# Local heads in 96-query blocks, strided heads by residue, and X in token order for an attention + MLP kernel

## The chip, the cores and the metric

The kernel runs on one core of a Trainium2 chip. The metric is the time of one execution on the device in microseconds (us). Every time below is a median of several executions, with the lowest and highest beside it. The engines are named as the profile names them: PE is TensorE (matmuls), PEld its loads of the stationary operand, DVE is VectorE, ACT is ScalarE, POOL is GpSimd, and SP is SyncE, which only issues DMAs here.

Executions of the kernel before differ by up to about 3% on one chip. Each execution has a state: it is called slow when it is over 1.5% above the fastest one of the same kernel.

## The reference

Eight batches of 8 heads, 576 positions, head width 64. Heads 0 to 3 see a local window of 32 positions, heads 4 to 7 see every 32nd position. The result, 4608 tokens of 512 features, goes through an MLP (512 to 2048 to 512) with a rational activation. It is condensed here to its core, not quoted:

```python
mask_local   = (rel >= 0) & (rel < 32)                      # heads 0..3
mask_strided = (rel >= 0) & (pos_k % 32 == pos_q % 32)      # heads 4..7
attn = softmax(where(mask, q @ k.T / 8, -1e9)) @ v
x = attn.transpose(0, 2, 1, 3).reshape(4608, 512)
h = x @ w_in                                                # 512 -> 2048
P = a0 + a1*h + a2*h*h + a3*h*h*h
Q = 1 + |b0|*|h| + |b1|*h*h
out = (P / (Q + 1e-6)) @ w_out                              # 2048 -> 512
```

## The kernel before

The program records its operations and puts them into a fixed order for each engine. For each batch there are score rounds (`scores`), five attention tiles (`attend`), and then one MLP chunk of 512 tokens (`dense1`, activation, `dense2`, `store`). The last 64 tokens of all eight batches form a ninth chunk.

Attention produces X with tokens on partitions (`XR`). The MLP needs it transposed, with features on partitions and tokens along the free dimension. A transposing DMA does this, tile by tile, into `XT`:

```python
# attend(b), tile T of five
ev = add("SP", (lambda e, dst=dst, x=x: e.dma_start_transpose(dst, x[:, :])),   # dst = XT[b % 2][:, :, 128*T : 128*T+128]
         [o3, wait], 1.25, key - 60, gx, 0.6)
```

The first dense layer then runs four matmuls for each block of 128 hidden features, one for each 128 input features. `r` is the moving operand (512 columns, one a token), and all of them are read in the order in which they lie:

```python
# dense1(c)
for kk in range(NK1):                                    # NK1 = 4
    if c < 8:
        r = XT[c % NXT][:, kk, :]
    else:
        r = XT8[:, kk, :].rearrange("x (n c) -> x n c", c=32)[:, :, 0:16]
    makers.append(mm(psH[hi], Win[:, kk, 128 * f:128 * f + 128], r, kk == 0, kk == NK1 - 1))
```

To get this the kernel keeps the queries of each 128-token tile in the order (residue mod 4, position). The copy of the transposed queries out of PSUM puts them in that order, and `store` undoes it with four DMAs for each tile. The copy of the transposed keys writes `kL` in token order, in steps of 4 elements:

```python
# scores(b), turn_l: queries, then keys
e = [(eng, qL[:, a, 0:512].rearrange("x (t g p) -> x g t p", t=4, g=4),
      lambda ps, a=a: ps[:, a, :].rearrange("x (g t p) -> x g t p", g=4, t=4), 512) for a in range(2)]
e = [(eng, kL[:, :, 0:512].rearrange("x a (p g) -> x a g p", g=4),
      lambda ps: ps.rearrange("x a (g p) -> x a g p", g=4), 1024)]
# ... (cut)
# store(c, m): rows in steps of 4
dst = out[576 * c + 128 * m:576 * c + 128 * m + 128, :].rearrange("(p g) o -> g p o", g=4)
for g in range(4):
    add("SP", (lambda e, dst=dst, osl=osl, g=g: e.dma_start(
        dst[g], OS[osl][32 * g:32 * g + 32, :])), [ev], 0.75, key - 60, go, 0.2)
```

The softmax here doesn't subtract the row's maximum and nothing guards it: scores larger than these inputs give would overflow.

## Time and profile before

| | before |
|---|---|
| median (lowest to highest), 3 runs | 435.72 us (430.99 to 436.88) |
| profiled span, mean granted clock of TensorE | 435.9 us, 0.930 |
| first matmul of the first dense layer | 45.4 us |
| steady stage | 180 to 340 us, about 40 us a chunk (39.7 to 41.9 from start to start between 178 and 300 us) |
| issue of the last 32 stores | 14.9 us |

These are lines of the profile page before. The first gives for each engine its busy time, its share of the span and its instructions. In the others, each digit is the busy share of one fortieth of the span in tenths; PEclk is the granted clock of TensorE in tenths, and DMA is the mean busy share of the 16 DMA engines.

```profile
PE 367.6 (84%) x3417; PEld 175.6 (40%) x3417; DVE 329.0 (75%) x309; ACT 305.4 (70%) x338; POOL 107.4 (25%) x144
...
PE   6751877679996999799989999999999997998760
...
DVE  3421197960599589689996989796989999999920
ACT  2320398926794899789978897879897798849510
...
PEclk9875698969999999999999999999999999899895
DMA  9999998029929923952594265221123101012012
```

The start is thin on PE, DVE and ACT while the DMA engines are nearly full for the first seven slices (76 us); the middle is full on PE, DVE and ACT together, and the end is thin again. So three engines share the steady stage, and the start and the tail are waits.

Two groups of instructions on the page before. The columns are line, engine, operation, written and read tiles, shape and count, then busy us and mean ns of one, then the idle time of the engine before them and what ended it.

```profile
L518 PE MATMUL psH<-XT,Win 128*128 128x512 bf16 x576 | 147.5, 393 | 18.9 <-DMA XT<-XR 16.8
...
L813 ACT ACTIVATE HB<-psH 128x512 bf16<-128x512 f32 x144 | 84.3, 600 | 58.8 <-PE psH L518 57.7
```

The mean of a matmul (393 ns) contains a modelled end and overlaps its neighbours. What it costs in a full stream is read from starts. The PE timeline before, with start, duration, and runs of equal instructions folded:

```profile
305.15 1.03 PE L518 MATMUL psH<-XT,Win 128*128 128x512 bf16 x4
306.02 1.03 PE L518 MATMUL psO<-Wout,T 128*128 128x512 bf16 x4
306.88 1.03 PE L518 MATMUL psH<-XT,Win 128*128 128x512 bf16 x4
```

Four matmuls take 306.02 - 305.15 = 0.87 us, so one takes about 216 ns. The next view is the table of windows. Its columns are the window, its length, the busy us and count of PE, PEld, DVE, ACT and POOL, the granted clock, the DMA share and GB/s.

```profile
180.00:220.00 40.00, 37.25 (x401) 18.66 (x400) 34.74 (x32) 36.40 (x39) 13.23 (x17) 1.00 0.57 78
...
300.00:340.00 40.00, 39.84 (x326) 18.84 (x325) 38.59 (x32) 32.96 (x39) 0.00 (x0) 1.00 0.21 50
```

PE has no slack, and DVE and ACT have little slack. The start is in the chain of waits (start us, us, what), and PE's list of waits (total us, times, longest) gives the sum:

```profile
27.13 8.14 DMA XT<-XR
36.09 9.20 DMA XT<-XR
45.38 6.34 PE psH L518 x16
```

```profile
PE psH L518 <- DMA XT<-XR: 16.8, 4, 7.9
```

Two transposing DMAs in a row hold up the first dense matmul. The median one of the run lands 2.4 us after its issue, and these two take 8.1 and 9.2 us at a time when the DMA engines are nearly full; that the loads delay them is likely, but was not tested. The tail is on SP's timeline:

```profile
419.18 14.93 SPq L874 DMA_DIRECT2D out_dram<-OS  x32
```

Last, the groups of ACT's copies out of PSUM, with shapes kept apart:

```profile
L529 ACT ACTIVATE kL<-psS 128x1024 bf16<-128x1024 f32 x6 | 14.8, 2464 | 1.8 <-PE psS L518 1.8
...
L529 ACT ACTIVATE sT<-psS 128x1024 bf16<-128x1024 f32 x6 | 6.1, 1020 | 0.0
```

Both copies move 1024 elements per partition. The one that writes SBUF in 8-byte steps (`kL`) takes 2.4 times as long as the one that writes in order (`sT`).

### The profile page before, as it was taken

What the parts mean: (1) busy time and instruction counts of PE and PEld (TensorE: products, weight loads), DVE (VectorE), ACT (ScalarE), POOL (GpSimd) and SP (SyncE); (2) the same over time, 40 slices, a digit from 0 to 9 for tenths busy, and PEclk for the clock granted to TensorE, in tenths of its full rate; (3) what the DMA queues carried; (4) which work ended last, traced back from release to release, by engine and by line L of the source; (5) the groups of instructions that cost most, each with busy time, mean ns of one, the idle gap of its engine ahead of it and who ended that gap; (6) DMA issues with size and microseconds to landing.
All of it is one profiled execution on the core that took longest, in us unless ns stands there. A gap on an engine that the chain in (4) does not pass through costs nothing.

```text
span 435.9 us, 7966 instructions
## 1 busy us (share of the span) xinstructions
PE 367.6 (84%) x3417; PEld 175.6 (40%) x3417; DVE 329.0 (75%) x309; ACT 305.4 (70%) x338; POOL 107.4 (25%) x144
## 2 busy tenths in 40 slices
PE   6751877679996999799989999999999997998760
PEld 2330332334552454355435444553454442343320
DVE  3421197960599589689996989796989999999920
ACT  2320398926794899789978897879897798849510
POOL 9985211008208402900580064000000000000000
PEclk9875698969999999999999999999999999899895
DMA  9999998029929923952594265221123101012012
GB/s 130 182 192 166 199 110 108 15 29 96 115 54 127 94 49 47 147 81 50 67 149 74 48 85 69 61 50 26 26 48 85 28 23 48 25 44 54 24 35 64
DMA packets 92260, 34.05 MB, mean 78 GB/s; under 512 B 66112, under 2 KB 87104, under 8 KB 92224
## 3 DMA queue, kind: packets, MB, share of 16 engines
q0 software_dynamic: 62144, 18.37, 42.0%
q1 hardware_dynamic: 30080, 15.16, 16.2%
q8 instruction: 27, 0.44, 0.5%
q14 instruction: 9, 0.07, 0.1%
HBM read 37.17 MB, written 9.44 MB: 107 GB/s over the span
## 4 chain that ended last, share of the span: by engine, by line
PE 49%; DVE 25%; DMA 11%; ACT 9%; issue 3%; SPq 1%; DVEq 0%
PE psH L518 20%; PE psO L518 14%; PE psS L518 10%; DMA XT<-XR 9%; PE psA L518 6%; DVE UU L827 4%; DVE T L852 3%; DVE T L843 3%; DVE T L847 3%; ACT kL L529 2%; DVE XR L749 2%; ACT UU L833 2%; DVE T L845 2%; DVE UU L824 2%; ACT UU L836 2%
## 5 line engine op out<-in xcount | busy, mean ns | idle before, releaser
L518 PE MATMUL psH<-XT,Win 128*128 128x512 bf16 x576 | 147.5, 393 | 18.9 <-DMA XT<-XR 16.8
L518 PE MATMUL psO<-Wout,T 128*128 128x512 bf16 x528 | 133.9, 384 | 8.7 <-ACT OS L917 4.9
L813 ACT ACTIVATE HB<-psH 128x512 bf16<-128x512 f32 x144 | 84.3, 600 | 58.8 <-PE psH L518 57.7
L518 PEld LDWEIGHTS psH<-XT,Win 128*128 128x128 bf16 x576 | 55.0, 100 | 87.0 <-issue 16.3
L833 ACT ACTIVATE UU<-UU,cst 128x2048 bf16<-128x2048 bf16 x36 | 71.5, 1998 | 7.1 <-DVE UU L827 7.0
L518 PEld LDWEIGHTS psO<-Wout,T 128*128 128x128 bf16 x528 | 47.1, 98 | 65.6 <-ACT OS L917 9.1
L836 ACT ACTIVATE UU<-UU 128x2048 bf16<-128x2048 bf16 x36 | 68.5, 1912 | 0.1
L821 DVE TENSOR_SCALAR T<-HB 128x4096 uint16<-128x4096 uint16 (+1 forms) x20 | 22.4, 1121 | 38.6 <-ACT HB L813 38.6
L852 DVE TENSOR_TENSOR T<-T,UU 128x4096 bf16<-128x4096 bf16 (+1 forms) x20 | 41.3, 2063 | 4.0 <-ACT UU L836 4.0
L485 POOL DMA_DIRECT2D vs<-in_v_dram x32 | 27.4, 861 | 63.9 <-PE psA L518 63.5
L847 DVE TENSOR_TENSOR T<-T,HB 128x4096 bf16<-128x4096 bf16 (+1 forms) x20 | 41.4, 2069 | 0.3
L827 DVE TENSOR_TENSOR UU<-UU,T 128x4096 bf16<-128x4096 bf16 (+1 forms) x20 | 41.4, 2069 | 0.3
L843 DVE TENSOR_TENSOR T<-T,HB 128x4096 bf16<-128x4096 bf16 (+1 forms) x20 | 41.3, 2067 | 0.2
L457 POOL DMA_DIRECT2D qn<-in_q_dram x9 | 8.7, 965 | 89.7 <-PE psS L518 88.9
L749 DVE TENSOR_TENSOR XR<-psA,RC 128x512 bf16<-128x512 f32 x40 | 27.4, 686 | 3.2 <-DMA XT<-XR 3.0
L917 ACT ACTIVATE OS<-psO 128x512 f32<-128x512 f32 x33 | 20.0, 606 | 12.7 <-PE psO L518 12.2
L495 POOL DMA_DIRECT2D vt<-in_v_dram x32 | 26.1, 847 | 0.0
L575 ACT ACTIVATE ES<-psS 128x864 bf16<-128x864 f32 (+1 forms) x20 | 17.0, 852 | 12.5 <-PE psS L518 11.0
L840 DVE TENSOR_SCALAR T<-HB,coef 128x4096 bf16<-128x4096 bf16 (+1 forms) x20 | 24.8, 1238 | 0.3
L824 DVE TENSOR_SCALAR UU<-T,coef 128x4096 bf16<-128x4096 bf16 (+1 forms) x20 | 24.6, 1230 | 0.3
L845 DVE TENSOR_SCALAR T<-T,coef 128x4096 bf16<-128x4096 bf16 (+1 forms) x20 | 23.6, 1182 | 0.3
L747 DVE RECIPROCAL RC<-psA 128x8 f32<-128x8 f32 x40 | 8.1, 203 | 20.8 <-PE psA L518 20.7
(111 smaller groups left out, 391.7 us busy)
## 6 DMA issues: line engine op xcount, KB each, us to landing
out_dram<-OS SPq DMA_DIRECT2D x128, 64.0 KB, 1.7
qn<-in_q_dram POOLq DMA_DIRECT2D x7, 512.0 KB, 6.8
kn<-in_k_dram POOLq DMA_DIRECT2D x7, 512.0 KB, 5.8
vs<-in_v_dram POOLq DMA_DIRECT2D x32, 64.0 KB, 6.3
vt<-in_v_dram POOLq DMA_DIRECT2D x32, 64.0 KB, 3.5
Win<-in_moe_w_in_dram POOLq DMA_DIRECT2D x1, 2048.0 KB, 13.4
Wout<-in_moe_w_out_dram POOLq DMA_DIRECT2D x1, 2048.0 KB, 26.2
out_dram<-OS SPq DMA_DIRECT2D x32, 32.0 KB, 1.7
```

Source lines behind the costliest of these rows:

```text
L485: add("POOL", (lambda e, b=b, i=i, h=h: e.dma_start(vs[i][:, h, :, 0:64], v[b, 4 + h, 0:512, :].rearrange("(p g) d -> p g d", g=4))), base ...
L518: return lambda e: e.matmul(out_ap, l, r, start=start, stop=stop, skip_group_check=True)
L749: o3 = add("DVE", (lambda d, rc=rc, x=x: d.tensor_tensor(x.rearrange("x (h d) -> x h d", h=8), psA[:, :, 0:64], rc[:, :, :].to_broadcast([ ...
L813: o2 = add("ACT", (lambda a, hb=hb, hi=hi, fi=fi: a.activation(hb[:, fi, :], psH[hi], AF.Copy)), [o1, hb_free[ig % NHB]], 0.6, key - HOFF)
L824: d2 = add("DVE", (lambda d, gn=gn, u=u, t3=t3: d.tensor_scalar(u[:, 0:gn, :], t3[:, 0:gn, :], b1_ap, b0_ap, op0=Alu.mult, op1=Alu.add)), ...
L827: d3 = add("DVE", (lambda d, gn=gn, u=u, t3=t3: d.tensor_tensor(u[:, 0:gn, :], u[:, 0:gn, :], t3[:, 0:gn, :], op=Alu.mult)), [d2], ctt, ke ...
L833: ln = add("ACT", (lambda a, u=u, sl=sl: a.activation(u[:, sl, :], u[:, sl, :], AF.Ln, bias=cst[:, 0:1], scale=1.0)), [d3, cons], 0.28 + H ...
L836: ex = add("ACT", (lambda a, u=u, sl=sl: a.activation(u[:, sl, :], u[:, sl, :], AF.Exp, scale=-1.0)), [ln], 0.28 + HG * CH * 0.000833, key ...
L843: d5 = add("DVE", (lambda d, gn=gn, hb=hb, t3=t3: d.tensor_tensor(t3[:, 0:gn, :], t3[:, 0:gn, :], hb[:, 0:gn, :], op=Alu.mult)), [d4], ctt ...
L845: d6 = add("DVE", (lambda d, gn=gn, t3=t3: d.tensor_scalar(t3[:, 0:gn, :], t3[:, 0:gn, :], a_ap[1], None, op0=Alu.add)), [d5], cts, key + ...
L847: d7 = add("DVE", (lambda d, gn=gn, hb=hb, t3=t3: d.tensor_tensor(t3[:, 0:gn, :], t3[:, 0:gn, :], hb[:, 0:gn, :], op=Alu.mult)), [d6], ctt ...
L852: d9 = add("DVE", (lambda d, gn=gn, t3=t3, u=u: d.tensor_tensor(t3[:, 0:gn, :], t3[:, 0:gn, :], u[:, 0:gn, :], op=Alu.mult)), [d8, lns], c ...
```

## The change

The intent was to shorten the start, to lighten PE a little in the steady stage, and to store each tile with one DMA. Its parts:

- Local heads run in six blocks of 96 queries against windows of 128 keys, so the correction matmuls between tiles go. Local and strided scores share five rounds instead of six.
- An attention tile of the strided heads holds the tokens of one residue mod 4, so 64 matmuls of 32 columns become 16 full ones.
- X of batches 0 and 1 is turned on TensorE (`XP = 2`) and copied by ACT; later batches still use transposing DMAs, now one for the local and one for the strided half. The strided q and k of batches from 2 on are turned by DMA too (`XD = 2`).
- The weights load in parts, and there are three X buffers instead of two.
- Everything after attention is in token order, so a tile needs one store DMA instead of four.

The local half of X (`XTl`) lies in token order, but the strided half (`XTs`) lies by residue: column 128 * g + p holds token 4 * p + g. Both halves are summed into the same PSUM columns. So the moving operand of two matmuls in four is read with p outside and g inside, and neighbouring columns are 128 bf16 elements, or 256 bytes, apart (32 elements, or 64 bytes, in the ninth chunk). Such a read is called hopped below, and one in the order in which the data lies a plain read. The diff, cut:

```diff
+    XD = 2
+    XP = 2
 ...
-    NXT = 2
-    XT = [A(f"XT{i}", [128, NK1, CH], BF) for i in range(NXT)]
-    XT8 = A("XT8", [128, NK1, B * 128], BF)
+    NXT = 3
+    XTl = [A(f"XTl{i}", [128, 2, CH], BF) for i in range(NXT)]
+    XTs = [A(f"XTs{i}", [128, 2, CH], BF) for i in range(NXT)]
+    XT8l = A("XT8l", [128, 2, B * 64], BF)
+    XT8s = A("XT8s", [128, 2, B * 128], BF)
 ... (96-query windows, mixed score rounds, weights in parts: cut)
+            dst = (kL[:, :, PADK:PADK + 512] if x else qL[:, :, 0:512]).rearrange("x a (p g) -> x a g p", g=4)
 ...
+            if T < 4:
+                stg = (XTs[xb][:, :, 128 * T:128 * T + 128], b)
+            elif T == 4:
+                stg = (XT8s[:, :, 128 * b:128 * b + 128], 8)
 ... (b < XP: four matmuls against the identity, ACT copies; else two transposing DMAs: cut)
@@ dense1 @@
-                    if c < 8:
-                        r = XT[c % NXT][:, kk, :]
+                    if kk < 2:
+                        r = XTl[c % NXT][:, kk, :] if c < 8 else XT8l[:, kk, :]
+                    elif c < 8:
+                        r = XTs[c % NXT][:, kk - 2, :].rearrange("x (g p) -> x p g", g=4)
                     else:
-                        r = XT8[:, kk, :].rearrange("x (n c) -> x n c", c=32)[:, :, 0:16]
+                        r = XT8s[:, kk - 2, :].rearrange("x (b g p) -> x b p g", b=B, g=4)[:, :, 0:16, :]
@@ store @@
-            dst = out[576 * c + 128 * m:576 * c + 128 * m + 128, :].rearrange("(p g) o -> g p o", g=4)
-            for g in range(4):
-                add("SP", (lambda e, dst=dst, osl=osl, g=g: e.dma_start(
-                    dst[g], OS[osl][32 * g:32 * g + 32, :])), [ev], 0.75, key - 60, go, 0.2)
+            add("SP", (lambda e: e.dma_start(out[576 * c + 128 * m:576 * c + 128 * m + 128, :], OS[osl][:, :])),
+                [ev], 0.75, key - 60, go, 0.9)
```

## The prediction

> **What bounds the kernel before.** Median 435.72 us; profiled span 435.9.
>
> - *Start.* The timeline shows the first dense matmul (psH) at 45.4 us, although batch 0's last attention tile is normalised near 36. The chain of waits fills 27.1 to 45.4 with two transposing DMAs (XT<-XR, 8.1 and 9.2 us). The granted clock is then 0.50.
> - *Early stage.* From 60 to 140 us PE is busy about 79% (table by windows). psH waits 16.8 us on transposed X in four waits, that at 45.4 included; chunk 1's first dense matmul comes at 102.5, chunk 2's at 139.7 after a 7.0 us transpose on the chain.
> - *Steady stage.* From 180 to 340 us PE is back to back at clock 1.00. A chunk takes 38 to 40 us: 128 dense matmuls at 216 ns start to start (27.7 us) and, from starts in the trace, about 10 us of attention. DVE is close behind (31 us dense, 6.8 attention per chunk), ACT also (about 37). From 340 DVE binds (39.8 of 40).
> - *End.* The last PE work starts near 420; SP then issues 32 stores for 14.9 us (SP's timeline).
>
> **What the change does, costed.**
>
> 1. X of batches 0 and 1 turned on PE: the two DMA waits before 45.4 go, replaced by four matmuls and two ACT copies (0.4 us each, estimate) per tile; six tiles instead of five, each about 2 us through the one psA. First dense matmul at about 38: -7 us. Chunk 1's wait goes too, and three XT buffers help: -6 us in 60 to 140.
> 2. PE per steady batch: the 16 residue transposes (0.9 us) go to a DMA; 64 32-column strided matmuls become 16 full ones; masks shrink 2.8 to 2.45 us; EL2's correction matmuls go. About -1.5 us.
> 3. ACT: five exps (4.9 us) for seven (5.6); sT copy gone (-1.0); but the query copy now writes with a 4-element step, which costs 2.46 us on kL (group table) where qL took 1.2. Net -0.4.
> 4. DVE: -1.2 (sT), +0.6 (sixth tile), +0.4 (small copies): about zero, so it limits what step 2 yields: -6 us over the run.
> 5. Stores: 4 to 1 per tile; the last 32 become 8, issued in about 5 us: -9 us at the end. More transposing DMAs (14 a batch for 5) stay off the critical path.
>
> Sum -27 us: about **409 us**.
>
> **Main risk.** dense1 now reads half its moving operands (XTs, 288 of 576 matmuls) as single bf16 elements 256 bytes apart. The Trainium skill's "SBUF — State Buffer" (section "Door 1: The DMA port swizzle") says SBUF has 16-byte cachelines and each access crossing to a new line pays a penalty. No matmul in this trace reads so; runs of 8 elements are the shortest. The nearest thing is the kL copy's 8-byte write step: 2.46 us against 1.02. Doubling those matmuls (+216 ns x 288 = 62 us) would give about 450. I think it likelier (70%) that the read is nearly free.
>
> **Range** 394 to 448 (8 in 10). Chances: faster by over 2% 0.72, within 2% 0.11, slower by over 2% 0.17.
>
> **What would show it.** First psH near 38 us; starts of psH<-XTs matmuls 216 ns apart (430 refutes me); steady chunk about 37 us; few waits on DMA XTl or XTs, under 3 us each; ACT qL copy about 2.46 us; DVE busy near 329 us; tail after the last matmul 7 us, not 15.
>
> **What would make it wrong.** The strided moving read; 96-column stationary loads slower than 128-column ones (98 ns in the trace); single-buffered sT now waiting on its DMA; ACT overloaded by X copies and strided copies in batches 0 and 1.

## The result, and the profile after

The changed kernel takes 611.32 us (609.98 to 613.17, 4 runs), against 436.3 us (430.99 to 438.07) for the kernel before. The ratio is 1.4071, with a 95% interval of 1.3933 to 1.421. Here and below a ratio is the mean time of one kernel's fast runs over that of the other's fast runs of the same rounds, so it is not quite the ratio of the medians.

The page after, the same lines as before:

```profile
PE 561.6 (92%) x2761; PEld 186.5 (31%) x2804; DVE 325.6 (54%) x324; ACT 318.8 (52%) x332; POOL 112.3 (18%) x156
...
PE   6589974899989999999999999999999989999996
...
DVE  3304649106474364656357736655653866284982
ACT  3424559335664526664647465656351672555652
...
PEclk9855765557995889998879998999987998899999
```

PE looks even busier (92% for 84%), yet DVE and ACT do about the same work as before at less density (54% and 52% busy, for 75% and 70%). The Trainium skill's "Perfetto Trace Analysis" (section "Identifying the Most-Contended Engine") says that the busy share of matmuls is not a good measure of how close a kernel is to the roofline, and names the share of weight loads as one of two to use instead. This trace agrees: PEld fell from 40% to 31% while PE rose. The groups name the place:

```profile
L508 PE MATMUL psH<-XTs,Win 128*128 128x512 bf16 x256 | 242.5, 1036 | 0.0
L817 ACT ACTIVATE HB<-psH 128x512 bf16<-128x512 f32 x144 | 85.1, 598 | 199.9 <-PE psH L508 199.8
...
L508 PE MATMUL psH<-XTl,Win 128*128 128x512 bf16 x242 | 88.3, 447 | 6.3 <-issue 2.4
```

The XTs and the XTl matmuls have the same shape, and the first are recorded at more than twice the duration. ACT, which copies each psH out, now idles 199.9 us on PE instead of 58.8. The PE timeline after shows the cost by starts:

```profile
300.17 0.59 PE L508 MATMUL psH<-XTl,Win 128*128 128x512 bf16 x2
300.60 1.89 PE L508 MATMUL psH<-XTs,Win 128*128 128x512 bf16 x2
302.31 1.04 PE L508 MATMUL psO<-Wout,T 128*128 128x512 bf16 x4
```

Two XTl matmuls take 0.43 us, or 215 ns each, as before. Two XTs matmuls take 302.31 - 300.60 = 1.71 us, or 855 ns each: four times as much. In the windows of the same place DVE and ACT starve while PE is as "busy" as it was:

```profile
180.00:220.00 40.00, 37.49 (x215) 12.37 (x212) 16.77 (x21) 20.14 (x21) 8.78 (x13) 0.79 0.68 76
...
300.00:340.00 40.00, 39.14 (x239) 13.77 (x242) 23.30 (x26) 24.69 (x24) 6.46 (x7) 0.91 0.23 40
```

In the first of these windows PE ran 215 matmuls instead of 401 in the same busy time. The chain of what ended last is now PE nearly throughout, where before it had DVE 25% and DMA 11%:

```profile
PE 88%; ACT 5%; DVE 3%; DMA 2%; issue 1%; POOL 0%; SPq 0%; POOLq 0%
```

The parts of the change that were meant to gain time do what they should. The PE timeline shows the first dense matmul at 36.2 us instead of 45.4, the waits of psH on X are down to one of 1.9 us, and SP's timeline shows a third of the issue time at the end:

```profile
36.20 0.63 PE L508 MATMUL psH<-XTl,Win 128*128 128x512 bf16 x1 [0.71 <-ACT XT8l L750]
```

```profile
PE psH L508 <- DMA XT8l<-XR: 1.9, 1, 1.9
```

```profile
600.83 5.04 SPq L874 DMA_DIRECT2D out_dram<-OS  x8
```

Where did the time go? All starts in the trace of the 288 matmuls that read in hops (XTs and XT8s) sum to 249.5 us. At 216 ns each they would take 62 us, so the read costs about 187 us. The rest of the loss goes with the clock: the clock records of both traces hold only 1.0 and 0.5 of full speed, and show 175.6 us at half clock, against 62.7 us before. Of the dense matmuls that read in order, 117 started at half clock (427 ns apart in full stream) after and 40 before, which is 77 x 0.21 = 16 us. That is an estimate: some records are missing, and the matmuls of attention are not counted. The hopped matmuls themselves hardly feel it: 870 ns in the median at half clock and 856 at full clock. So something other than the array sets their pace.

### The profile page after: what moved, and what is told of

It reads as the page before. It is cut to its first block, busy times and chain, and to the rows that moved or that the text cites. A ratio compares the mean times of both kernels' runs of the same rounds, so it can differ in the third digit from the quotient of the medians.

```text
span 608.2 us, 6669 instructions
## 1 busy us (share of the span) xinstructions
PE 561.6 (92%) x2761; PEld 186.5 (31%) x2804; DVE 325.6 (54%) x324; ACT 318.8 (52%) x332; POOL 112.3 (18%) x156
## 4 chain that ended last, share of the span: by engine, by line
PE 88%; ACT 5%; DVE 3%; DMA 2%; issue 1%; POOL 0%; SPq 0%; POOLq 0%
PE psH L508 54%; PE psO L508 20%; PE psS L508 8%; PE psA L508 6%; ACT kL L520 1%; DMA kn<-in_k_dram 1%; ACT UU L837 1%; ACT UU L840 1%; DMA XT8l<-XR 1%; DVE XR L721 1%; ACT OS L917 1%; DVE kL L521 0%; ACT qL L520 0%; ACT HB L817 0%; ACT E_0 L572 0%
## 5 line engine op out<-in xcount | busy, mean ns | idle before, releaser
L508 PE MATMUL psH<-XTs,Win 128*128 128x512 bf16 x256 | 242.5, 1036 | 0.0
L817 ACT ACTIVATE HB<-psH 128x512 bf16<-128x512 f32 x144 | 85.1, 598 | 199.9 <-PE psH L508 199.8
L508 PE MATMUL psO<-Wout,T 128*128 128x512 bf16 x505 | 139.8, 404 | 5.7 <-ACT OS L917 3.4
L508 PE MATMUL psH<-XTl,Win 128*128 128x512 bf16 x242 | 88.3, 447 | 6.3 <-issue 2.4
L719 DVE RECIPROCAL RC<-psA 128x8 f32<-128x8 f32 (+1 forms) x48 | 9.7, 203 | 117.6 <-PE psA L508 117.6
L477 POOL DMA_DIRECT2D vt<-in_v_dram x48 | 41.8, 906 | 116.0 <-PE psA L508 116.0
L508 PEld LDWEIGHTS psH<-XTl,Win 128*128 128x128 bf16 x256 | 24.6, 108 | 82.3 <-issue 48.7
L508 PEld LDWEIGHTS psH<-XTs,Win 128*128 128x128 bf16 x256 | 28.6, 112 | 41.8 <-issue 20.1
L721 DVE TENSOR_TENSOR XR<-psA,RC 128x512 bf16<-128x512 f32 (+1 forms) x48 | 30.9, 643 | 0.3
L508 PE MATMUL psH<-XT8s,Win 128*128 128x512 bf16 x32 | 29.9, 1024 | 0.0
L508 PE MATMUL psS<-M,IDN 128*128 128x480 bf16 (+1 forms) x69 | 23.2, 421 | 2.8 <-DVE sT L521 1.3
```

Of the source, the lines that this page charges most:

```text
L477: add("POOL", (lambda e, i=i, t=t, p0=p0, s0=s0: e.dma_start(vt[i][p0:128, t, :, 0:64], v[b, 0:4, s0:s0 + 128 - p0, :].rearrange("h p d -> ...
L508: return lambda e: e.matmul(out_ap, l, r, start=start, stop=stop, skip_group_check=True)
L721: o3 = add("DVE", (lambda d, rc=rc, x=x, nh=nh: d.tensor_tensor(x[:, 0:64 * nh].rearrange("x (h d) -> x h d", d=64), psA[:, 0:nh, 0:64], r ...
L817: o2 = add("ACT", (lambda a, hb=hb, hi=hi, fi=fi: a.activation(hb[:, fi, :], psH[hi], AF.Copy)), [o1, hb_free[ig % NHB]], 0.6, key - HOFF)
```

## The experiments

The theory is that the hopped moving read costs the whole loss. It has a mechanism: the 16-byte lines of the skill's "SBUF — State Buffer", with the price set by the number of times that the stream changes line. The rivals are that something else in the change costs the time (96-column weight loads, the new tiling, the lower clock); that the price comes from the 256-byte distance, a power of two (called C); or that any step other than one element is slow (D). All runs in one overview; "wrong" means that the kernel gives a wrong result. The range is that of all runs, the ratio is to the kernel before.

| run | result | us, median (lowest to highest) | ratio (95%) |
|---|---|---|---|
| e1_plain_read | wrong | 407.7 (407.0 to 409.81) | 0.9476 (0.9386 to 0.9567) |
| e2_before_hops | wrong | 608.26 (600.2 to 614.43) | 1.4014 (1.3729 to 1.4298) |
| e3_patterns | wrong | 499.76, one look | none |
| e4_psum_hops | correct | 463.48 (460.36 to 466.77) | 1.0775 (1.0606 to 1.0943) |
| e5_pool_copy | correct | 412.97 (411.29 to 417.91) | 0.9531 (0.9491 to 0.9571) |
| e6_dve_copy | correct | 419.01 (417.27 to 422.47) | 0.9689 (0.9632 to 0.9746) |
| e7_pool_swap | correct | 405.06 (401.56 to 406.04) | 0.9339 (0.9292 to 0.9387) |
| e8_plain_xp0 | wrong | 429.86 (429.38 to 430.22) | 0.9926 (0.9874 to 0.9979) |
| e9_st_on_pe | correct | 406.25 (405.05 to 406.69) | 0.9446 (0.9376 to 0.9517) |
| e10_tail_32 | correct | 411.83 (409.12 to 415.24) | 0.9577 (0.9489 to 0.9664) |
| e11_before_swap | correct | 425.16 (422.86 to 435.37) | 0.9858 (0.9788 to 0.9927) |

The runs e1 to e4 shared one chip, e5 to e8 a second call, e9 to e11 a third. The kernel before had medians of 435.03, 434.03 and 433.25 us in these. Two of the four runs of e2, one of the six of e5 and two of the six of e11 were slow; the ratios leave them out.

### The changed kernel with a plain read

```diff
-                        r = XTs[c % NXT][:, kk - 2, :].rearrange("x (g p) -> x p g", g=4)
+                        r = XTs[c % NXT][:, kk - 2, :]
                     else:
-                        r = XT8s[:, kk - 2, :].rearrange("x (b g p) -> x b p g", b=B, g=4)[:, :, 0:16, :]
+                        r = XT8s[:, kk - 2, :].rearrange("x (n c) -> x n c", c=32)[:, :, 0:16]
```

The two halves of X then belong to different tokens, so the result is wrong (relative error 0.046), but every instruction count and size is the same.

> The changed kernel, but dense1 reads the strided heads' X (XTs, XT8s) in the order in which it lies, without hops. Wrong result on purpose (columns of the two halves do not match); everything else is as in the change. Theory A (the hop read alone costs 288 x 650 ns = 187 us, and the clock that falls while PE waits for its reads some 20 us more): about 405 to 415 us, matmuls of XTs 216 ns start to start, granted clock back to 0.93 or more. Rival B (the loss is spread: smaller transposing DMAs, single sT buffer, extra ACT copies, low clock of other origin): stays above 450 us although those matmuls are short.

Measured: 407.7 us, and a granted clock of 0.934. The view by tile gives the durations (lowest, median, highest in ns) and the first and last start. First after, then this run:

```profile
L508 PE MATMUL psH<-XTs,Win x256: 1021/1042/1051, 36.6 to 526.9; 128*128 128x512 bf16 x128
```

```profile
L508 PE MATMUL psH<-XTs,Win x256: 378/379/634, 38.7 to 338.6; 128*128 128x512 bf16 x128
```

Start to start they are back at 216 ns. Chunks start 36 to 38 us apart in the steady stage, for about 60 us after. One address pattern is worth 611.3 - 407.7 = 203.6 us, which the 187 us of reads and the 16 us of clock nearly fill. (The same 288 matmuls sum to 70.2 us by their starts here, 179 us less than after, so 8 us more stay unassigned if one compares the two traces directly.) The rest of the change is a gain.

### The kernel before with hops

```diff
-                        r = XT[c % NXT][:, kk, :]
+                        r = XT[c % NXT][:, kk, :] if kk < 2 else XT[c % NXT][:, kk, :].rearrange("x (g p) -> x p g", g=4)
```

This does the suspected part alone, on the kernel before (chunks 0 to 7, 256 matmuls). The result is wrong.

> The kernel before, with one edit: the matmuls of kk 2 and 3 of dense1 in chunks 0 to 7 read XT in hops of 256 bytes (256 matmuls). Wrong result on purpose. Theory A: 256 x 650 ns = 166 us more plus a lower clock, so 590 to 625 us. Rival B: the hop read is dear only together with the changed buffers, so clearly less than 560 us.

Measured: 608.26 us; the two fast runs took 600.2 and 606.67, for a ratio of 1.4014. The PE timeline has the pair of hopped matmuls at the pace seen after, (321.17 - 319.46) / 2 = 0.855 us each:

```profile
319.46 1.89 PE L518 MATMUL psH<-XT,Win 128*128 128x512 bf16 x2
321.17 1.04 PE L518 MATMUL psO<-Wout,T 128*128 128x512 bf16 x4
```

The 256 hopped matmuls sum to 223.0 us by their starts, 168 us more than at 216 ns, and the mean of the fast runs moved by 173 us (603.4 against 603.4 / 1.4014 = 430.6). So the read alone, without new tiles, 96-column loads, or new DMAs, makes the loss. The granted clock fell here too (0.904 in this profile, 0.930 before), so the fall of the clock comes with the read and not with the other parts.

### Sixteen patterns in one kernel

```diff
-                        r = XTs[c % NXT][:, kk - 2, :]
+                        r = hop(XTs[c % NXT], kk - 2, 2 * c + f % 2)   # pattern 0..15, 16 matmuls each
```

Starting from the plain read, each half of the blocks of a chunk reads in its own pattern. Each matmul still has 512 columns. The result is wrong.

> A measurement, wrong result on purpose: the changed kernel with sixteen read patterns of the moving operand XTs, two per chunk (even and odd f), looked at as start-to-start times of 512-column matmuls. Line theory (one 16-byte line is fetched per 1.69 ns, so what counts is lines touched per column): runs of 2 elements 430 ns, of 4, 8, 16 216 ns; steps of 4 bytes 216, of 8 bytes 430, of 16 and 32 bytes 865; hops of 264 or 272 bytes still 865; 2 or 16 streams instead of 4 still 865. Rival C (conflict of hops at a power of two): hops of 264 or 272 bytes fall to 216. Rival D (any read that isn't unit step is slow): steps of 4 bytes and runs of 4 also 865.

Measured: medians of 16 from start to start, taken from the trace. The first and the second matmul of a pair differ by some 20 ns (846 and 865 for the hop of the change), so the median of 16 lies between the two. "Changes" counts by hand how often two neighbouring columns lie in different 16-byte lines, in 512 columns.

| moving read of 512 bf16 | changes of line | ns start to start |
|---|---|---|
| in order (two patterns) | 64 | 215 and 215 |
| 4 streams 256 bytes apart, runs of 1 (two patterns) | 512 | 865 and 856 |
| 4 streams, runs of 2 | 256 | 438 |
| 4 streams, runs of 4 | 128 | 224 |
| 4 streams, runs of 8 | 64 | 216 |
| 4 streams, runs of 16 | 64 | 216 |
| step of 4 bytes | 128 | 227 |
| step of 8 bytes | 256 | 442 |
| step of 16 bytes | 512 | 900 |
| step of 32 bytes | 512 | 917 |
| 4 streams 264 bytes apart, runs of 1 | 512 | 858 |
| 4 streams 272 bytes apart, runs of 1 | 512 | 858 |
| 16 streams 64 bytes apart, runs of 1 | 512 | 848 |
| 2 streams 512 bytes apart, runs of 1 | 512 | 483 |

The PE timeline of chunk 6 has the last two rows: a pair with 16 streams takes 1.70 us from its start to the next one's, and a pair with 2 streams 0.97.

```profile
354.82 1.87 PE L508 MATMUL psH<-XTs,Win 128*128 128x512 bf16 x2
356.52 1.04 PE L508 MATMUL psO<-Wout,T 128*128 128x512 bf16 x4
...
357.83 1.13 PE L508 MATMUL psH<-XTs,Win 128*128 128x512 bf16 x2
358.80 1.03 PE L508 MATMUL psO<-Wout,T 128*128 128x512 bf16 x4
```

In all rows but the last the price follows the changes of line: 865 / 512 = 1.69 ns each, so 256 changes cost 433 (438 and 442 measured) and 128 cost 216, which a read in order takes anyway. C falls, since distances of 264 and 272 bytes cost the same as 256. D falls, since steps of 4 bytes and runs of 4 are nearly free. The theory does not explain the last row: two alternating streams change line at every column and cost only 483, where 865 was expected. So the count of line changes fits these reads but is not shown to be the mechanism. That stays open.

The Trainium skill's "SBUF — State Buffer" (section "Door 1: The DMA port swizzle") says that two hits per 16-byte line are needed to absorb the latency, and that one can stride for free as far as 8 bf16 elements. For a matmul's moving operand these runs differ: two hits per line (a step of 8 bytes) cost 442 ns for 216, a step of 8 elements cost 900, and four hits per line are needed. The measurement decides.

### The hop on the PSUM side

```diff
-                        r = XTs[c % NXT][:, kk - 2, :].rearrange("x (g p) -> x p g", g=4)
+                        r = XTs[c % NXT][:, kk - 2, :]
+                    o = psH[hi]
+                    if kk >= 2:
+                        o = o.rearrange("x (p g) -> x g p", g=4)
```

Reading in order and writing the sums into PSUM in steps of 4 fp32 gives the right result without any copy (the edit for chunk 8 is alike).

> Right result. The permutation is moved from the read of XTs to the write of psH: the matmuls of kk 2 and 3 read contiguously and write their 512 columns to PSUM in steps of 16 bytes. If a stepped PSUM write is free: as e1, 405 to 415 us. If it costs as the read did (4 times): about 610 us. The Trainium skill's Advanced Engine Details page says that a non-contiguous PSUM pattern slows matmuls significantly, so I expect 430 to 610 us.

Measured: 463.48 us, correct. Those matmuls start 429 ns apart in the median, twice the normal time. By tile:

```profile
L508 PE MATMUL psH<-XTs,Win x256: 591/634/1142, 37.4 to 389.1; 128*128 128x512 bf16 x128
```

Moving the reordering to the output halves the spacing from 865 to 429 ns but still costs 463.5 - 407.7 = 55.8 us against the plain read, and leaves the kernel slower than before. The skill's "Advanced Engine Details and Errata" (section "Memory Cachelines") says that any non-contiguous pattern in PSUM significantly slows down matmuls. This trace agrees, and gives the size for a 16-byte step: twice. Two things set this slowdown apart from that of the read. The seven of these matmuls that started at half clock took 733 to 854 ns, so this pace follows the clock, and the hopped read's did not (870 and 856). And the granted clock did not fall: 0.947 in this profile.

### A copy into token order, on POOL

```diff
+    XTn = [A(f"XTn{i}", [128, 2, CH], BF) for i in range(NXT)]
 ...   # b >= 2, once the four strided tiles of the batch have landed
+                        cp = add("POOL", (lambda e: e.tensor_copy(
+                            XTn[xb].rearrange("x k (p g) -> x k p g", g=4),
+                            XTs[0].rearrange("x k (g p) -> x k p g", g=4))), [list(sg), xt_free[xb]], 2.5, key - 60)
 ...
-                        r = XTs[c % NXT][:, kk - 2, :].rearrange("x (g p) -> x p g", g=4)
+                        r = XTn[c % NXT][:, kk - 2, :]
```

One copy a batch replaces 32 slow reads of the same data. In batches 0 and 1 the ACT copies that exist anyway write in token order directly.

> Right result, meant to beat both kernels. The permutation is paid once per batch instead of once per matmul: POOL, idle most of the time, copies XTs (128 x 1024) into natural order for batches 2 to 7; for batches 0 and 1 the ACT copies out of PSUM write in steps of 8 bytes. dense1 reads contiguously. Theory A: as the kernel with the plain read (407.7 us), plus at most a few us if the copy (estimate 1 to 2.5 us) ends on the critical path: 405 to 418 us. If POOL's copies slow DVE (its 4096-element products then above 2.28 us) or come late behind POOL's own DMA issues: above 420 us.

Measured: 412.97 us, correct, ratio 0.9531. The groups of POOL and ACT:

```profile
L523 ACT ACTIVATE qL<-psS 128x1024 bf16<-128x1024 f32 x8 | 19.8, 2479 | 7.9 <-PE psO L511 6.5 <-PE psS L511 1.4
...
L779 POOL COPY XTn<-XTs 128x1024 bf16<-128x1024 bf16 x6 | 14.8, 2459 | 99.5 <-DMA XTs<-XR 99.5
```

POOL pays about 2.5 us a batch, where PE paid 32 x 0.65 = 21 us for the hops of one chunk. The change, so repaired, beats the kernel before. DVE's busy time rose from 323.6 us in the plain read to 331.1 here with no DVE instruction added, and the trace shows where: the DVE instructions that overlap one of POOL's copies in time are together 7.9 us longer than the median of their kind, and all others together 0.3 us shorter. Three products of 2.28 us, for instance, took 3.5 to 3.9 us beside a copy. So the copy on POOL is not free for DVE, as the expectation had feared, though the total stayed within its 405 to 418 us.

### The same copy on DVE

```diff
-                        cp = add("POOL", (lambda e: e.tensor_copy(
+                        cp = add("DVE", (lambda e: e.tensor_copy(
```

> Right result. As the POOL copy, but the same copies on DVE, which is the busiest engine after PE (80% in the plain-read run). Six copies of 1 to 2.3 us plus eight small ones: DVE busy up by 8 to 16 us, time 2 to 10 us above the POOL copy.

Measured: 419.01 us, 6.0 us more than on POOL, though DVE is twice as fast at it:

```profile
L779 DVE COPY XTn<-XTs 128x1024 bf16<-128x1024 bf16 x6 | 7.6, 1273 | 4.4 <-DMA XTs<-XR 4.4
```

DVE is full in the later stage, and here it also idles 4.4 us for the transposing DMA before the copy. DVE's busy time in all is the same in both runs (330.9 us here, 331.1 with the copy on POOL), so it isn't added work that costs the 6 us. POOL has room. That the place in DVE's order is what costs the 6 us is argued, not shown.

### Swapping the sides of the step in the q and k copies

```diff
-            dst = (kL[:, :, PADK:PADK + 512] if x else qL[:, :, 0:512]).rearrange("x a (p g) -> x a g p", g=4)
+            dst = (kL[:, :, PADK:PADK + 512] if x else qL[:, :, 0:512]).rearrange("x a (p g) -> x a p g", g=4)
 ...
-                [x], "l", [(eng, dst, lambda ps: ps.rearrange("x a (g p) -> x a g p", g=4), 1024)], [l_old, ini[id(kL)]])
+                [x], "l", [(eng, dst, lambda ps: ps.rearrange("x a (g p) -> x a p g", g=4), 1024)], [l_old, ini[id(kL)]])
```

The copy moves the same elements to the same places. Only its order differs: it now writes SBUF in order and reads PSUM in hops of 512 bytes. The rest is the kernel with the POOL copy.

> Right result. The POOL copy, and the evacuations of qL and kL walk in the other order: they write contiguously and read PSUM in hops of 512 bytes, instead of reading contiguously and writing in steps of 8 bytes (2.46 us each). If only stepped SBUF writes are slow: 1.02 us each, ACT busy down by about 20 us over the run and 1 to 6 us off the time. If hops are slow on the PSUM read too: 2 us or more each and no gain.

Measured: 405.06 us, correct, ratio 0.9339. This is the best kernel and beats both given ones.

```profile
L523 ACT ACTIVATE qL<-psS 128x1024 bf16<-128x1024 f32 x8 | 8.3, 1041 | 7.9 <-PE psO L511 6.5 <-PE psS L511 1.4
...
L523 ACT ACTIVATE kL<-psS 128x1024 bf16<-128x1024 f32 x6 | 6.1, 1024 | 2.8 <-PE psS L511 2.8
```

The copy fell from 2479 to 1041 ns, as fast as a copy with both sides in order (1020). ACT's hopped read of PSUM is nearly free here, and its stepped write of SBUF is not. ACT's busy time fell from 315.0 to 295.7 us, and 412.97 - 405.06 = 7.9 us of that reached the span.

### The same swap on the kernel before

```diff
-                e = [(eng, kL[:, :, 0:512].rearrange("x a (p g) -> x a g p", g=4),
-                      lambda ps: ps.rearrange("x a (g p) -> x a g p", g=4), 1024)]
+                e = [(eng, kL[:, :, 0:512].rearrange("x a (p g) -> x a p g", g=4),
+                      lambda ps: ps.rearrange("x a (g p) -> x a p g", g=4), 1024)]
```

> Right result. The kernel before with one edit: kL is evacuated with contiguous writes and hopped PSUM reads. The copy falls from 2.46 to 1.02 us. The chain before has 2.2% (9.6 us) of ACT kL on it; as PE is what binds in the steady stage I expect 2 to 8 us less than before (ratio 0.98 to 0.995).

Measured: 425.16 us in the median; the four fast runs took 422.86 to 426.01, ratio 0.9858. Two lines are worth 1.4% on the kernel as it stood.

```profile
L529 ACT ACTIVATE kL<-psS 128x1024 bf16<-128x1024 f32 x6 | 6.2, 1036 | 1.8 <-PE psS L518 1.8
```

### Plain read without turning X on TensorE

```diff
-    XP = 2
+    XP = 0
```

This is the plain read (result wrong) with X of every batch turned by DMA.

> The plain-read kernel (wrong result on purpose), with X of all batches turned by DMA (XP = 0), so without the part that turns X of two batches on TensorE. My prediction's step 1 put that part at 13 us together with the XT buffers: about 415 to 421 us here and the first dense matmul at 43 to 46 us, against 407.7 us and 37.9.

Measured: 429.86 us. The first dense matmul starts at 52.3 us instead of 37.9, and PE's waits show why:

```profile
PE psH L508 <- DMA XT8l<-XR: 17.8, 4, 10.3
```

So turning X of two batches on TensorE is worth about 429.86 - 407.7 = 22 us by the medians, and about 19 us by the ratios (0.9926 and 0.9476). The prediction had 13 for it, and the expectation above missed both of its numbers. It does more than remove the old waits: without it the start would be later than before (52.3 us against 45.4). In this run's chain to the first dense matmul SP's issuing of the DMAs takes 4.1 us, which the chain before does not have. That the second DMA of each tile is what delays the start is likely, but was not tested.

### The strided q and k turned on TensorE, and the tail with 32 stores

Both start from the best kernel.

```diff
-    XD = 2
+    XD = 8
```

> Right result. The best version so far (POOL copy, swapped evacuations), with the residue transposes of q and k (sT) of all batches back on TensorE (XD = 8). My step 2 said that moving them to a DMA frees 0.9 us of PE per batch, and steps 3 and 4 that it frees 1.0 us of ACT and 1.2 us of DVE: so 3 to 9 us slower than 405.06 us. If the sT DMAs cost as much in waits as they free: within 2 us of it.

Measured: 406.25 us against 405.06. It was run at another time. By the medians the DMA of strided q and k is worth 1.2 us. By the ratios it is 1.1%, or nearly 5 us, because the fast runs of the kernel before differed. It is not settled beyond 0 to 5 us.

```diff
-                add("SP", (lambda e, r0=r0, bb=bb: e.dma_start(out[r0:r0 + 64, :], OS[osl][64 * bb:64 * bb + 64, :])),
-                    [ev], 0.6, key - 60, go, 0.5)
+                for g in range(4):
+                    add("SP", (lambda e, r0=r0 + 16 * g, p0=64 * bb + 16 * g: e.dma_start(
+                        out[r0:r0 + 16, :], OS[osl][p0:p0 + 16, :])), [ev], 0.45, key - 60, go, 0.1)
```

> Right result. The same best version, with the last chunk's eight stores cut into 32 of 16 rows, as the kernel before has them. My step 5 put this at 9 us: 414 us, SP issuing for about 15 us at the end instead of 5. If the end hides it: 405 us.

Measured: 411.83 us. SP's timeline has the old tail again:

```profile
392.32 14.68 SPq L897 DMA_DIRECT2D out_dram<-OS  x32
```

The issue takes 9.7 us more than the 5.02 us of the eight stores, of which 411.83 - 405.06 = 6.8 us reach the end by the medians (5.6 against the run just above). By the ratios it is 2.4%, or some 10 us. The traces side with the larger figure: from the (modelled) end of the last matmul to the end of the run it is 14.5 us here and 5.4 us in the best kernel. This profile is 4 us ahead already at the first weight load of chunk 3 (160.1 us for 164.3), long before the edited stores, so that lead is not the edit's.

## Why the prediction was wrong

The prediction was 409 us with a range of 394 to 448, and the kernel takes 611. The step that failed is the one headed "Main risk": "I think it likelier (70%) that the read is nearly free". The read costs 650 ns a matmul, 187 us in all. In its place the runs show a read that paces the matmul: 865 ns for 216, and 203.6 us off the time when it alone is made plain. The fallback in the same paragraph failed too: "Doubling those matmuls (+216 ns x 288 = 62 us) would give about 450" took the pace of a stepped write in ACT as the measure, but a read with one element per line costs four times the normal pace, not twice. The evidence was on the table: the skill's page said that each crossing to a new line pays, and the kL copy showed 2.4 times for two elements per line. With one element per line, the price of a crossing had to be taken at every column. That the ACT write and the matmul read share a cause is not shown.

Point by point:

- First dense matmul near 38 us: right. It is at 36.2 after and at 37.9 with the plain read. The moment varies by chance: the kernel before with hops, edited only from that matmul on, has 41.0 for 45.4, and the sixteen patterns have 41.8.
- XTs matmuls 216 ns apart, "430 refutes me": refuted, 865 in the median of all 288 (855 in the lines shown).
- Steady chunk about 37 us: about 60 after, 36 to 38 with the plain read. The step was right apart from the read.
- Waits on X under 3 us: right, one of 1.9. The query copy at 2.46 us: right, 2.470. DVE busy near 329: right, 325.6. Tail after the last matmul 7 us, not 15: 5.4 for 14.7, and the issue of the last stores fell from 14.9 to 5.0 us as expected.
- The sum without the read: 409 predicted, 407.7 measured with the plain read. That it is so near is in part luck. The prediction subtracts 27 us from 435.72, and in the call of the plain read the fast runs of the kernel before took 430.6 in the mean: by these the gain is 22.5 us (430.6 to 408.1). And its parts were less exact: turning X on TensorE brought 19 to 22 us for 13, and the stores 6 to 10 for 9, so nothing is left for the other steps, which had 6.
- "96-column stationary loads slower": no harm seen, since the plain read keeps them and lands near the sum. "Single-buffered sT" and "ACT overloaded": the same. None of the three was tested by itself.
- Not foreseen: the granted clock fell with the slow reads, which cost about 16 us more. The skill's "TensorE: Matmul & The Clock Gate" (Part 1) says that the clock is halved when the array is not busy enough. That a PE waiting for its reads counts as not busy enough fits both hopped runs (0.857 after, 0.904 in the kernel before with hops, against 0.930 and 0.934 with plain reads), but it is inferred; no run tests it. It does not hold for every slow matmul: with the stepped writes to PSUM, which take twice as long, the clock stayed at 0.947.

## What to carry to other kernels

Count, for the innermost order in which a matmul reads its moving operand, how often the stream changes to another 16-byte line; at the 1.69 ns a change seen here, four bf16 elements per line are nearly free and one element per line costs four times (two alternating streams were the exception, at 483 ns). If a layout must be reordered, do it once, on an engine with slack (whose work can still slow a neighbour, as POOL's copies did DVE) and with the step on the side where it is free (a PSUM read in ACT), rather than in each of the many matmuls that reuse the data. And when a change carries one access pattern that the old trace never shows, price it at its worst case, or widen the range to hold it.

## What the Trainium skill lacked or had wrong

- "SBUF — State Buffer" (section "Door 1: The DMA port swizzle") gives no size for a change of line, and its free distance is too generous for a matmul: 512 moving bf16 columns cost 216 ns in order, 224 to 227 with four elements per 16-byte line, 438 to 442 with two, and 848 to 917 with one. Two alternating streams cost only 483, which its rule does not explain.
- "TensorE: Matmul & The Clock Gate" (section "Back-to-back issue gap") gives the spacing of matmuls by columns, weight loads and clock, and not by how the moving operand is read. For 512 columns it has about 216 ns for a matmul alone and about 131 ns in a stream with weight loads. Here such a stream ran at 216 ns with reads in order, never near 131, and at 865 ns with hopped ones, at either clock (870 and 856).
- "TensorE: Matmul & The Clock Gate" (Part 1) does not say how a PE that waits for its operand reads counts for the clock gate; here the mean granted clock fell from 0.930 to 0.857 with PE shown busy 92%.
- "Advanced Engine Details and Errata" (section "Memory Cachelines") does not size the slowdown of stepped PSUM writes (429 ns for 216 at a 16-byte step, and 733 to 854 at half clock).
- No page has the cost of a stepped copy out of PSUM by ACT: a copy of 1024 elements that writes SBUF in 8-byte steps takes 2.46 us, and one that instead reads PSUM in hops of 512 bytes takes 1.02 to 1.04 us, like one in order on both sides (1.02). DVE behaved alike in its one such copy a run (2.43 and 1.23 us).
